# Weights of the last stage split sooner, one unit's weight sums on VectorE, and tokens loaded ahead of weights

## The chip, the cores and the metric

The kernel runs on one core of a Trainium2 chip. The metric is device time in microseconds, the median of several executions of the whole program; lower is better. Times inside the program come from one profiled execution, counted in us from the start of its span.

## What is computed

```python
scores = q @ k.T / sqrt(64) - log(448)         # 8 x 12 heads, 448 x 64 each, fp32
x = sigmoid(scores) @ v                        # tokens: 8*448 = 3584, features: 12*64 = 768
h = maximum(maximum(x @ w1, x @ w2), x @ w3)   # each w is 768 x 768
out = h @ w_out                                # 768 x 768
```

Everything is fp32. The weights arrive as 64-bit patterns (`w123`, `wout`), which the kernel decodes itself.

## The kernel before

First comes the attention (up to about 260 us), then the four products with weights. The change touches only the second part, at the step to its last stage.

The second part is a list of 16 **visits** (`visits`): four **stages** (three for column blocks of w1, w2 and w3, with the maximum taken among the three; the fourth, `LAST`, is w_out) times four **pairs** of batches. A visit has three **units** (q = 0, 1, 2), each a product of a 768 x 256 piece of weights with 768 x 896 tokens, done in Strassen's manner (Winograd's form): seven block **products** (k = 0 to 6, `PRODUCTS`) on 2 x 2 blocks. I write (n, q, k) for visit, unit, product, as the code does. Visit 12 is the first of the last stage.

A product (`product`, line 439 before) is nine matmuls 128 x 128 by 448. fp32 accuracy comes from splitting each operand in a rounded part and a remainder: three blocks of the contraction times `whi*xhi`, `whi*xlo` and `wlo*xhi`. So every operand needs a cast on ScalarE (`whi`, `xhi`) and a subtraction on VectorE (`wlo`, `xlo`, lines 154 and 264). The operands of the seven products are partly sums: of weights, `s1` to `s4` (`W_SUMS`, `w_combine`), and of tokens, `t1` to `t4` (`x_combine`, line 229, three 448-wide steps each). Both kinds of sum run on GpSimd. `s3` and `t3` overwrite the blocks a21 and b12.

Every engine's order is that of the program text (`pin`). What is done after which product stands in small tables with keys (n, q, k):

- `ws` says after which product a weight operand is split (`w_split`: cast, then remainder). Its list `when` has a row for each unit.
- `w_loads` says when the four weight blocks of a unit are loaded (`w_load`): unit 1 of the next stage where the last split of unit 0 stands, unit 2 where the last split of unit 1 stands. The loads go on SP's one queue, in the order a21, a22, a11, a12, and the four sums follow at the same place on GpSimd.
- `his` and `los` say when tokens are cast and when their remainder is taken; those of the next visit stand after the products of unit 2, and the last three after products of the next visit's unit 0.
- the tokens of the next visit are loaded by `x_load`: four loads on SP and then twelve steps on GpSimd. In the last stage this stands after (n, 0, 4), but in visit 12 after (12, 0, 6), behind the weight loads.

All staging tiles (`ws_*`, `xs_*`) and split tiles (`whi_*`, `wlo_*`, `xhi_*`, `xlo_*`) have one buffer each, so a load waits for the last reader of what it overwrites. The products accumulate in PSUM banks; bank 2 takes product 3 and again product 6 of a unit, and its results `m22` and `m12` are read by VectorE in between (`put`, line 511), before the bank is written again.

The line that sets the splits of unit 0, and the place of the token load:

```python
when = [[(n - 1, 1, 4 + k // 3) for k in range(7)],        # unit 0
        [(n, 0, 1)] * 2 + [(n, 0, 4)] * 2 + [(n, 0, 5)] * 2 + [(n, 0, 6)],   # unit 1
        [(n, 1, 4 + k // 3) for k in range(7)]]            # unit 2
...
if here == (n, 0, 6 if (n, 0, 6) in w_loads else 4) and nst in (0, LAST):
    xs = x_load(x_dram if nst == 0 else h_dram, np_)
```

Of the kernel before, what the change touches and what calls it, by code (L numbers as in the profile page):

```python
# [39 lines left out]
def attention_then_maxout(  # L40
# [31 lines left out]
    nc = tc.nc  # L72
# [8 lines left out]
    pin = tc.keep_in_program_order  # L81
# [52 lines left out]
        "s4": ("a12", "s2", ALU.subtract),  # L134
    }

    def w_combine(r, names):
        for name in names:
            r[name] = r["a21"] if name == "s3" else ws_p.tile([P, HP], F32, name=f"ws_{name}")
            in0, in1, op = W_SUMS[name]  # L140
            pin(nc.gpsimd.tensor_tensor(out=r[name], in0=r[in0], in1=r[in1], op=op))  # L141

    def w_load(st, q):
        r = w_stage()
        for name, sums in W_ORDER:
            pin(nc.sync.dma_start(out=r[name], in_=w_dram[st, q][:, BLOCKS.index(name)]))
        for name, sums in W_ORDER:
            w_combine(r, sums)
        return r

    def w_split(q, name, r, copy):
# [111 lines left out]
    def x_lo(name, x, hi, lo):  # L263
        pin(nc.vector.tensor_tensor(out=lo, in0=x, in1=hi.bitcast(F32), op=ALU.subtract))  # L264
        x_ops[name] = hi, lo
# [180 lines left out]
    pairs = list(range(B // 2))  # L446
# [7 lines left out]
    for n in range(1, done):  # L454
        (st0, p0), (st, p) = visits[n - 1], visits[n]
        if st != st0:
            if st < LAST:
                when = [[(n - 1, 1, k // 2) for k in range(7)],
                        [(n - 1, 2, 2 + k // 2) for k in range(7)],
                        [(n, 0, 3 + k // 2) for k in range(6)] + [(n, 1, 0)]]  # L460
            else:
                when = [[(n - 1, 1, 4 + k // 3) for k in range(7)],
                        [(n, 0, 1)] * 2 + [(n, 0, 4)] * 2 + [(n, 0, 5)] * 2 + [(n, 0, 6)],
                        [(n, 1, 4 + k // 3) for k in range(7)]]
            for q in range(3):
                for key, (name, _, _) in zip(when[q], PRODUCTS):
                    ws.setdefault(key, []).append((q, name))
            w_loads[n - 2, 0, 0] = st, 0
            w_loads[when[0][-1]] = st, 1
            w_loads[when[1][-1]] = st, 2  # L470
        if (st == LAST, p) != (st0 == LAST, p0):
            for k, (_, name, _) in enumerate(PRODUCTS):
                his[n - 1, 2, k] = name
            keys = [(n - 1, 2, k) for k in range(1, 5)] + [(n, 0, k) for k in (0, 2, 3)]
            for key, (_, name, _) in zip(keys, PRODUCTS):
                los[key] = name
    w_next, split = {}, {}
# [17 lines left out]
    for n, (st, p) in enumerate(visits):  # L495
        nst, np_ = visits[n + 1] if (n, 2, 0) in his else (None, None)
        if nst in (1, 2):
            xs = x_load_all(np_)
        m = {}
        for q in range(3):  # L500
            ps, p1, u2, u3 = {}, None, None, None

            def put(name, y, add):

                y = y[:, :S]
                if st == LAST or q == 0:
                    m[name] = m_p.tile([P, S], F32, name=f"m{name}")
                    if add is None:
                        pin(nc.scalar.copy(out=m[name], in_=y))  # L509
                    else:  # L510
                        pin(nc.vector.tensor_tensor(out=m[name], in0=y, in1=add, op=ALU.add))  # L511
                elif add is None:
                    pin(nc.vector.tensor_tensor(out=m[name], in0=y, in1=m[name], op=ALU.max))
                else:
                    c = c_p.tile([P, S], F32, name="c")
                    pin(nc.vector.tensor_tensor(out=c, in0=y, in1=add, op=ALU.add))
                    pin(nc.vector.tensor_tensor(out=m[name], in0=c, in1=m[name], op=ALU.max))  # L517
                if st == LAST or q == 2:
                    half, t = int(name[0]) - 1, (2 * p + int(name[1]) - 1) * S
                    if st == LAST:  # L520
                        row = (q + 3 * half) * P
                        dst = outT[row : row + P, t : t + S]
                    else:
                        dst = h_dram[half][:, st, t : t + S]
                    pin(nc.sync.dma_start(out=dst, in_=m[name]))

            for k, (wname, xname, bank) in enumerate(PRODUCTS):
                here = n, q, k
                first = k < 4 or bank == 1
                if first:  # L530
                    ps[bank] = ps_y.tile(
                        [P, 512], F32, name=f"ps_y{bank}", bufs=2 if bank < 2 else 1
                    )
                product(ps[bank], w_ops[q][wname], x_ops[xname], first)
                if k == 0:
                    p1 = c_p.tile([P, S], F32, name="p1", bufs=1)
                    pin(nc.scalar.copy(out=p1, in_=ps[0][:, :S]))  # L537
                elif k == 1:
                    u2 = c_p.tile([P, S], F32, name="u2", bufs=1)
                    pin(nc.vector.tensor_tensor(out=u2, in0=ps[1][:, :S], in1=p1, op=ALU.add))  # L540
                elif k == 2:
                    u3 = c_p.tile([P, S], F32, name="u3", bufs=1)
                    pin(nc.vector.tensor_tensor(out=u3, in0=ps[3][:, :S], in1=u2, op=ALU.add))
                elif k == 3:
                    put("22", ps[2], u3)
                elif k == 4:
                    put("11", ps[0], None)
                elif k == 5:
                    put("21", ps[1], u3)
                elif k == 6:  # L550
                    put("12", ps[2], u2)
                if here in his:
                    split[his[here]] = x_hi(his[here], x_first if n == q == 0 else xs)
                if here in los:
                    x_lo(*split.pop(los[here]))
                for uq, name in ws.get(here, ()):
                    w_split(uq, name, w_next[uq], nc.scalar.copy)
                if here in w_loads:
                    w_st, uq = w_loads[here]
                    w_next[uq] = w_load(w_st, uq)  # L560
                if here == (0, 0, 4):
                    finish(c_p, ("c", "c"))

                if here == (n, 0, 6 if (n, 0, 6) in w_loads else 4) and nst in (0, LAST):
                    xs = x_load(x_dram if nst == 0 else h_dram, np_)
                if here == (n, 2, 0) and nst == 0:
                    t_store(xs, np_)
                if here in decodes:
                    next(background)
# [41 lines left out]
```

## Time and profile before

| | us |
|---|---|
| median of 3 runs | 883.14 (882.99 to 884.2) |
| profiled execution, its own time | 882.73 |
| its span | 880.9 |
| TensorE busy | 870.7 |
| VectorE busy | 623.0 |
| ScalarE busy | 392.0 |
| GpSimd busy | 182.0 |

The span runs from the first to the last instruction of the profiled execution; its own time is a little longer. Busy time of matmuls includes their overlap with the next, so the spacing of matmul starts tells more than their duration. DVE is VectorE, ACT ScalarE, POOL GpSimd, PE TensorE, SP the engine that issues the DMAs.

### The profile page before, as it was taken

Reading aid. Unit: us, or ns where it says so; the run is one execution under the profiler, and the core shown is the slowest. Engines: PE = TensorE matmul, PEld = TensorE weight load, DVE = VectorE, ACT = ScalarE, POOL = GpSimd, SP = SyncE. Lnnn points to the kernel's source line nnn. Section 1 sums busy time; section 2 is a strip of 40 time slices with the busy share of each in tenths; the row PEclk is TensorE's granted clock in tenths of the full one; section 3 lists DMA queues with packets and bytes.
Section 4 is the critical chain, followed back from the end, with each engine's and each line's share of the span. In section 5 each row is a group of like instructions: output and inputs, shape, how many; then the busy total and the mean of one; then the engine's idle time right before and its main releaser. Section 6 shows DMA issues by size and latency. Waiting matters only on the chain. (4 is left out here: it accounts for less than half of the span.)

```text
span 880.9 us, 12944 instructions
## 1 busy us (share of the span) xinstructions
PE 870.7 (99%) x4842; PEld 693.3 (79%) x4842; DVE 623.0 (71%) x874; ACT 392.0 (45%) x499; POOL 182.0 (21%) x148
## 2 busy tenths in 40 slices
PE   8999999999999999999999999999999999999998
PEld 4444544444459999999999999999999998899997
DVE  4676668767866847678687788878778696836442
ACT  6777677766681413332353343235334252423320
POOL 0100022023003463502100010210001553760600
PEclk9999999999999999999999999999999999999999
DMA  6667666776747555314845642474472426162412
GB/s 244 214 230 231 228 242 208 245 274 224 232 162 259 184 202 193 147 51 152 296 161 192 242 147 81 153 283 179 173 270 100 157 74 219 72 210 93 170 72 84
DMA packets 74334, 161.87 MB, mean 184 GB/s; under 512 B 6944, under 2 KB 53792, under 8 KB 74272
## 3 DMA queue, kind: packets, MB, share of 16 engines
q1 hardware_dynamic: 74272, 161.05, 52.3%
q8 instruction: 38, 0.62, 0.3%
q14 instruction: 24, 0.20, 0.1%
HBM read 109.90 MB, written 51.12 MB: 183 GB/s over the span
## 5 line engine op out<-in xcount | busy, mean ns | idle before, releaser
L308 ACT ACTIVATE a<-ps_s,bias_s 128x896 f32<-128x896 f32 x168 | 156.1, 1007 | 77.9 <-PE ps_s L338 59.6
L439 PE MATMUL ps_y<-xhi_t,wlo_s 128*128 128x448 f32 x432 | 158.0, 366 | 0.1
L439 PE MATMUL ps_y<-xhi_t,whi_s 128*128 128x448 f32 x432 | 157.9, 366 | 0.0
L439 PE MATMUL ps_y<-xlo_t,whi_s 128*128 128x448 f32 x432 | 157.9, 366 | 0.0
L346 PE MATMUL ps_av<-a,v 128*64 128x448 f32 x576 | 118.6, 548 | 0.0
L439 PE MATMUL ps_y<-xhi_b,wlo_a 128*128 128x448 f32 x288 | 105.4, 366 | 0.0
L439 PE MATMUL ps_y<-xhi_b,whi_a 128*128 128x448 f32 x288 | 105.3, 366 | 0.0
L439 PE MATMUL ps_y<-xlo_b,whi_a 128*128 128x448 f32 x288 | 105.3, 366 | 0.0
L141 POOL TENSOR_TENSOR ws_s<-ws_a,ws_a 128x384 f32<-128x384 f32 x12 | 15.1, 1262 | 414.4 <-DMA ws_a<-w_dram 317.8
L537 ACT COPY p<-ps_y 128x448 f32<-128x448 f32 x48 | 25.5, 531 | 158.1 <-PE ps_y L439 158.1
L439 PEld LDWEIGHTS ps_y<-xhi_t,wlo_s 128*128 128x128 f32 x432 | 81.3, 188 | 6.7 <-ACT xhi_b L260 0.5
L439 PEld LDWEIGHTS ps_y<-xlo_t,whi_s 128*128 128x128 f32 x432 | 81.3, 188 | 6.3
L439 PEld LDWEIGHTS ps_y<-xhi_t,whi_s 128*128 128x128 f32 x432 | 81.2, 188 | 6.3
L346 PEld LDWEIGHTS ps_av<-a,v 128*64 128x64 f32 x576 | 37.2, 136 | 59.4 <-issue 58.2
L511 DVE TENSOR_TENSOR m<-ps_y,u 128x448 f32<-128x448 f32 x72 | 44.6, 620 | 54.7 <-PE ps_y L439 54.7
L229 POOL TENSOR_TENSOR xs_t<-xs_b,xs_t 128x448 f32<-128x448 f32 x48 | 64.5, 1369 | 35.3 <-DMA xs_b<-x_dram 34.2
L509 ACT COPY m<-ps_y 128x448 f32<-128x448 f32 x24 | 12.8, 533 | 126.3 <-PE ps_y L439 120.1
L264 DVE TENSOR_TENSOR xlo_t<-xs_t,xhi_t 128x1344 fp32r<-128x1344 f32 x42 | 67.7, 1612 | 1.9 <-ACT xhi_t L260 1.9
L540 DVE TENSOR_TENSOR u<-ps_y,p 128x448 f32<-128x448 f32 x48 | 29.9, 622 | 54.8 <-PE ps_y L439 53.6
L264 DVE TENSOR_TENSOR xlo_b<-xs_b,xhi_b 128x1344 fp32r<-128x1344 f32 x42 | 66.9, 1593 | 0.0
L260 ACT CAST xhi_t<-xs_t 128x1344 fp32r<-128x1344 f32 x42 | 55.5, 1322 | 16.3 <-PE ps_y L439 7.9
L175 ACT ACTIVATE c<-wraw 128x384 f32<-128x384 f32 x48 | 27.0, 562 | 76.9 <-DVE m L517 46.4
(65 smaller groups left out, 1629.0 us busy)
## 6 DMA issues: line engine op xcount, KB each, us to landing
qk<-qk SPq DMA_DIRECT2D x48, 448.0 KB, 5.2
xs_b<-x_dram SPq DMA_DIRECT2D x30, 672.0 KB, 6.8
wraw<-w SPq DMA_DIRECT2D x36, 384.0 KB, 4.9
xs_t<-t_dram SPq DMA_DIRECT2D x18, 672.0 KB, 8.0
v<-v SPq DMA_DIRECT2D x24, 448.0 KB, 3.8
h_dram<-m SPq DMA_DIRECT2D x48, 224.0 KB, 1.9
xs_b<-h_dram SPq DMA_DIRECT2D x16, 672.0 KB, 6.2
outT<-m SPq DMA_DIRECT2D x48, 224.0 KB, 1.9
```

Of the source, the lines that this page charges most:

```text
L141: pin(nc.gpsimd.tensor_tensor(out=r[name], in0=r[in0], in1=r[in1], op=op))
L175: pin(nc.scalar.activation(out=square, in_=high.bitcast(F32), func=AF.Square))
L229: pin(nc.gpsimd.tensor_tensor(out=r[name][:, k], in0=r[in0][:, k], in1=r[in1][:, k], op=ALU.subtract))
L260: pin(nc.scalar.copy(out=hi, in_=r[name]))
L264: pin(nc.vector.tensor_tensor(out=lo, in0=x, in1=hi.bitcast(F32), op=ALU.subtract))
L308: pin(nc.scalar.activation(out=a, in_=ps[:, :, :S], func=AF.Sigmoid, bias=bias_s, scale=scale))
L346: pin(nc.tensor.matmul(ps[e * D : (e + 1) * D, :S], vt[:, (g * C + c) * 2 + e], a[:, e], start=c == 0, stop=False,))
L439: pin(nc.tensor.matmul(ps[:, :S], wt[:, k * P : (k + 1) * P], xt[:, k], start=first and n == 0, stop=n == len(terms) - 1, skip_group_check ...
L509: pin(nc.scalar.copy(out=m[name], in_=y))
L511: pin(nc.vector.tensor_tensor(out=m[name], in0=y, in1=add, op=ALU.add))
L537: pin(nc.scalar.copy(out=p1, in_=ps[0][:, :S]))
L540: pin(nc.vector.tensor_tensor(out=u2, in0=ps[1][:, :S], in1=p1, op=ALU.add))
```

## The change

Four edits at the step to the last stage.

1. The splits of unit 0 of the last stage stand after (11, 1, 1) to (11, 1, 4) and not after (11, 1, 4) to (11, 1, 6). With them the weight load of unit 1, whose place is that of the last of these splits, goes from (11, 1, 6) to (11, 1, 4).
2. The weight load of unit 2 of the last stage comes without its sums (`combine=False`).
3. These four sums are VectorE's, after (12, 1, 3).
4. The tokens of visit 13 are loaded after (12, 0, 4), ahead of the weight load of unit 2 at (12, 0, 6).

```diff
-    def w_combine(r, names):
+    def w_combine(r, names, engine=None):
         for name in names:
             r[name] = r["a21"] if name == "s3" else ws_p.tile([P, HP], F32, name=f"ws_{name}")
             in0, in1, op = W_SUMS[name]
-            pin(nc.gpsimd.tensor_tensor(out=r[name], in0=r[in0], in1=r[in1], op=op))
-
-    def w_load(st, q):
+            engine = engine or nc.gpsimd
+            pin(engine.tensor_tensor(out=r[name], in0=r[in0], in1=r[in1], op=op))
+
+    def w_load(st, q, combine=True):
...
         for name, sums in W_ORDER:
-            w_combine(r, sums)
+            if combine:
+                w_combine(r, sums)
...
             else:
-                when = [[(n - 1, 1, 4 + k // 3) for k in range(7)],
+                when = [[(n - 1, 1, 1 + k // 2) for k in range(7)],
...
+                if here == (done - len(pairs), 1, 3):
+                    for name in W_SUMS:
+                        w_combine(w_next[2], (name,), nc.vector)
...
-                    w_next[uq] = w_load(w_st, uq)
+                    w_next[uq] = w_load(w_st, uq, (w_st, uq) != (LAST, 2))
...
-                if here == (n, 0, 6 if (n, 0, 6) in w_loads else 4) and nst in (0, LAST):
+                if here == (n, 0, 4) and nst in (0, LAST):
```

How this moves instructions stands in the two programs' orders. The names carry a running number at their end; `wlo_a11_0` is the remainder of block a11 for unit 0.

VectorE in unit 1 of visit 11, before:

```order
L540 TENSOR_TENSOR u2_6806<-ps_y1_6796,p1_6794 128x448
L543 TENSOR_TENSOR u3_6818<-ps_y3_6808,u2_6806 128x448
L516 TENSOR_TENSOR c_6830<-ps_y2_6820,u3_6818 128x448
L517 TENSOR_TENSOR m22_6724<-c_6830,m22_6724 128x448
L513 TENSOR_TENSOR m11_6736<-ps_y0_6784,m11_6736 128x448
L154 TENSOR_TENSOR wlo_a11_0_6844<-ws_a11_6361,whi_a11_0_6843 128x384
L154 TENSOR_TENSOR wlo_s2_0_6848<-ws_s2_6371,whi_s2_0_6847 128x384
L154 TENSOR_TENSOR wlo_s3_0_6852<-ws_a21_6363,whi_s3_0_6851 128x384
```

and now:

```order
L542 TENSOR_TENSOR u2_6806<-ps_y1_6796,p1_6794 128x448
L156 TENSOR_TENSOR wlo_a11_0_6809<-ws_a11_6361,whi_a11_0_6808 128x384
L156 TENSOR_TENSOR wlo_s2_0_6813<-ws_s2_6371,whi_s2_0_6812 128x384
L545 TENSOR_TENSOR u3_6826<-ps_y3_6816,u2_6806 128x448
L156 TENSOR_TENSOR wlo_s3_0_6829<-ws_a21_6363,whi_s3_0_6828 128x384
L156 TENSOR_TENSOR wlo_s1_0_6833<-ws_s1_6369,whi_s1_0_6832 128x384
L518 TENSOR_TENSOR c_6846<-ps_y2_6836,u3_6826 128x448
L519 TENSOR_TENSOR m22_6724<-c_6846,m22_6724 128x448
L156 TENSOR_TENSOR wlo_a12_0_6850<-ws_a12_6362,whi_a12_0_6849 128x384
L156 TENSOR_TENSOR wlo_a22_0_6854<-ws_a22_6364,whi_a22_0_6853 128x384
```

The remainders of unit 0 stand between the results of products 1 to 4 (`u2`, `u3`, `c`, `m22`), where they stood behind `m11` of product 4.

SP's queue from the first store of visit 12 on, before:

```order
L525 DMA outT<-m22_7080 128x448
L525 DMA outT<-m11_7093 128x448
L525 DMA outT<-m21_7114 128x448
L525 DMA outT<-m12_7134 128x448
L146 DMA ws_a21_7143<-w_dram32_98 128x384
L146 DMA ws_a22_7144<-w_dram32_98 128x384
L146 DMA ws_a11_7141<-w_dram32_98 128x384
L146 DMA ws_a12_7142<-w_dram32_98 128x384
L218 DMA xs_b11_7156<-h_dram0_66 128x3x448
L218 DMA xs_b12_7158<-h_dram0_66 128x3x448
L218 DMA xs_b22_7160<-h_dram1_67 128x3x448
L218 DMA xs_b21_7162<-h_dram1_67 128x3x448
```

and now:

```order
L527 DMA outT<-m22_7080 128x448
L527 DMA outT<-m11_7093 128x448
L220 DMA xs_b11_7104<-h_dram0_66 128x3x448
L220 DMA xs_b12_7106<-h_dram0_66 128x3x448
L220 DMA xs_b22_7108<-h_dram1_67 128x3x448
L220 DMA xs_b21_7110<-h_dram1_67 128x3x448
L527 DMA outT<-m21_7137 128x448
L527 DMA outT<-m12_7157 128x448
L147 DMA ws_a21_7166<-w_dram32_98 128x384
L147 DMA ws_a22_7167<-w_dram32_98 128x384
L147 DMA ws_a11_7164<-w_dram32_98 128x384
L147 DMA ws_a12_7165<-w_dram32_98 128x384
```

The four token loads have gone ahead of two stores and of the four weight loads.

VectorE from the end of product 3 of unit 1 in visit 12, before:

```order
L511 TENSOR_TENSOR m22_7225<-ps_y2_7215,u3_7213 128x448
L154 TENSOR_TENSOR wlo_a11_2_7241<-ws_a11_7141,whi_a11_2_7240 128x384
L154 TENSOR_TENSOR wlo_s2_2_7245<-ws_s2_7151,whi_s2_2_7244 128x384
L154 TENSOR_TENSOR wlo_s3_2_7249<-ws_a21_7143,whi_s3_2_7248 128x384
L511 TENSOR_TENSOR m21_7262<-ps_y1_7252,u3_7213 128x448
L154 TENSOR_TENSOR wlo_s1_2_7266<-ws_s1_7149,whi_s1_2_7265 128x384
```

and now:

```order
L513 TENSOR_TENSOR m22_7218<-ps_y2_7208,u3_7206 128x448
L142 TENSOR_TENSOR ws_s1_7221<-ws_a21_7166,ws_a22_7167 128x384
L142 TENSOR_TENSOR ws_s2_7223<-ws_s1_7221,ws_a11_7164 128x384
L142 TENSOR_TENSOR ws_a21_7166<-ws_a11_7164,ws_a21_7166 128x384
L142 TENSOR_TENSOR ws_s4_7226<-ws_a12_7165,ws_s2_7223 128x384
L156 TENSOR_TENSOR wlo_a11_2_7241<-ws_a11_7164,whi_a11_2_7240 128x384
L156 TENSOR_TENSOR wlo_s2_2_7245<-ws_s2_7223,whi_s2_2_7244 128x384
L156 TENSOR_TENSOR wlo_s3_2_7249<-ws_a21_7166,whi_s3_2_7248 128x384
L513 TENSOR_TENSOR m21_7262<-ps_y1_7252,u3_7206 128x448
```

The four sums stand ahead of the first remainder of unit 2's weights.

## Rows read from the trace of the kernel before

**Rows 1.** The head of the page: the span, and the busy time, share of the span and instructions of TensorE.

```profile
span 880.9 us, 12944 instructions
...
PE 870.7 (99%) x4842; PEld 693.3 (79%) x4842; DVE 623.0 (71%) x874; ACT 392.0 (45%) x499; POOL 182.0 (21%) x148
```

**Rows 2.** Who waited for whom, TensorE's matmuls alone, from 690 us to the end: us in total, times, longest us.

```profile
PE ps_y L439 <- DVE m L511: 1.4, 1, 1.4
PE ps_y L439 <- DVE xlo_t L264: 1.0, 1, 1.0
```

**Rows 3.** TensorE in order of time: start, duration, line, operation, operands; in brackets the idle time before and what ended it. The first matmul of visit 11, of visit 12, of unit 2 of visit 12, then the one with the longest wait, and the first of visits 13 and 14.

```profile
681.68 0.37 PE L439 MATMUL ps_y<-xhi_b,wlo_a 128*128 128x448 f32 x1
...
719.98 0.36 PE L439 MATMUL ps_y<-xhi_b,wlo_a 128*128 128x448 f32 x1
...
746.93 0.36 PE L439 MATMUL ps_y<-xhi_b,wlo_a 128*128 128x448 f32 x1
...
759.41 0.48 PE L439 MATMUL ps_y<-xhi_b,wlo_s 128*128 128x448 f32 x1 [1.38 <-DVE m L511]
...
761.36 0.36 PE L439 MATMUL ps_y<-xhi_b,wlo_a 128*128 128x448 f32 x1
...
800.48 0.36 PE L439 MATMUL ps_y<-xhi_b,wlo_a 128*128 128x448 f32 x1
```

**Rows 4.** VectorE in order of time, same columns: four remainders of visit 12's tokens (b11, t3, t1, t4).

```profile
713.26 1.55 DVE L264 TENSOR_TENSOR xlo_b<-xs_b,xhi_b 128x1344 fp32r<-128x1344 f32 x1
...
718.40 2.37 DVE L264 TENSOR_TENSOR xlo_t<-xs_b,xhi_t 128x1344 fp32r<-128x1344 f32 x1
...
721.23 1.83 DVE L264 TENSOR_TENSOR xlo_t<-xs_t,xhi_t 128x1344 fp32r<-128x1344 f32 x1
...
728.84 1.55 DVE L264 TENSOR_TENSOR xlo_t<-xs_t,xhi_t 128x1344 fp32r<-128x1344 f32 x1
```

**Rows 5.** SP in order of time, same columns, issues next to each other put together: visit 12's first four stores, unit 2's weight loads, the tokens of visit 13; then the tokens of visit 14.

```profile
730.94 4.74 SPq L525 DMA_DIRECT2D outT<-m  x4
...
735.77 1.83 SPq L146 DMA_DIRECT2D ws_a<-w_dram  x4
...
737.66 3.40 SPq L218 DMA_DIRECT2D xs_b<-h_dram  x4
...
772.63 2.73 SPq L218 DMA_DIRECT2D xs_b<-h_dram  x4
```

**Rows 6.** GpSimd in order of time, same columns: the first of unit 2's weight sums, the first and the last three token steps for visit 13, the first three for visit 14.

```profile
738.96 1.02 POOL L141 TENSOR_TENSOR ws_s<-ws_a,ws_a 128x384 f32<-128x384 f32 x1 [17.32 <-DMA ws_a<-w_dram]
...
745.89 4.01 POOL L229 TENSOR_TENSOR xs_t<-xs_b,xs_b 128x448 f32<-128x448 f32 x3 [2.40 <-DMA xs_b<-h_dram]
...
759.78 4.71 POOL L229 TENSOR_TENSOR xs_t<-xs_b,xs_t 128x448 f32<-128x448 f32 x3
...
779.32 3.36 POOL L229 TENSOR_TENSOR xs_t<-xs_b,xs_b 128x448 f32<-128x448 f32 x3 [14.83 <-DMA xs_b<-h_dram]
```

**Rows 7.** VectorE in order of time, same columns: remainders of unit 2's weights in visit 12 and the `m12` behind two of them.

```profile
744.50 0.56 DVE L154 TENSOR_TENSOR wlo_a<-ws_a,whi_a 128x384 fp32r<-128x384 f32 x1 [2.22 <-ACT whi_a L153]
...
747.38 2.93 DVE L154 TENSOR_TENSOR wlo_a<-ws_a,whi_a 128x384 fp32r<-128x384 f32 x2
...
750.24 0.61 DVE L511 TENSOR_TENSOR m<-ps_y,u 128x448 f32<-128x448 f32 x1
```

**Rows 8.** VectorE in order of time, same columns: results of products 2 and 3 of unit 1 of visit 11, the remainders of a12 and a22 of unit 0, and the result of product 1 of unit 2.

```profile
700.12 0.62 DVE L543 TENSOR_TENSOR u<-ps_y,u 128x448 f32<-128x448 f32 x1 [1.14 <-PE ps_y L439]
...
701.94 0.62 DVE L516 TENSOR_TENSOR c<-ps_y,u 128x448 f32<-128x448 f32 x1 [1.20 <-PE ps_y L439]
...
710.13 1.02 DVE L154 TENSOR_TENSOR wlo_a<-ws_a,whi_a 128x384 fp32r<-128x384 f32 x2
...
712.73 0.62 DVE L540 TENSOR_TENSOR u<-ps_y,p 128x448 f32<-128x448 f32 x1
```

**Rows 9.** GpSimd in order of time, same columns: the first and the last three token steps for visit 12, and the first weight sum of unit 1.

```profile
692.86 3.38 POOL L229 TENSOR_TENSOR xs_t<-xs_b,xs_b 128x448 f32<-128x448 f32 x3 [24.96 <-DMA xs_b<-h_dram]
...
703.70 4.44 POOL L229 TENSOR_TENSOR xs_t<-xs_b,xs_t 128x448 f32<-128x448 f32 x3
...
713.81 1.88 POOL L141 TENSOR_TENSOR ws_s<-ws_a,ws_a 128x384 f32<-128x384 f32 x1 [5.67 <-DMA ws_a<-w_dram]
```

**Rows 10.** ScalarE in order of time, same columns: the copy that gives m11 in unit 0 of visit 12.

```profile
729.30 0.53 ACT L509 COPY m<-ps_y 128x448 f32<-128x448 f32 x1 [5.94 <-PE ps_y L439]
```

**Rows 11.** DMA issues of a narrow stretch: destination and source, how many, KB each, median us from issue to landing. Issued at 772.63, 773.25 and 774.61 (tokens), at 775.76 and 776.21 (stores), from 653.82 to 655.42 (weights, behind token loads).

```profile
xs_b<-h_dram SPq DMA_DIRECT2D x1, 672.0 KB, 4.6
...
xs_b<-h_dram SPq DMA_DIRECT2D x1, 672.0 KB, 5.9
...
xs_b<-h_dram SPq DMA_DIRECT2D x1, 672.0 KB, 8.3
...
outT<-m SPq DMA_DIRECT2D x2, 224.0 KB, 7.8
...
ws_a<-w_dram SPq DMA_DIRECT2D x4, 192.0 KB, 8.9
```

**Rows 12.** Busy time by stretch: TensorE, its weight loads, VectorE, ScalarE and GpSimd, each with its instructions; then the granted TensorE clock, the share of the DMA engines, GB/s.

```profile
702.00:730.00 28.00, 27.46 (x136) 25.14 (x134) 27.79 (x33) 11.74 (x13) 13.89 (x9) 1.00 0.19 62
757.80:759.40 1.60, 0.24 (x2) 0.00 (x0) 1.56 (x2) 0.00 (x0) 1.60 (x1) 1.00 0.00 0
```

## The prediction

> **What bounds the kernel now.** I read the page first: TensorE is busy 870.7 of 880.9 us [rows 1], so a change to the order of side work can only give back, or take, time in which TensorE stands still. Next the waits of TensorE from 690 us on: only two of any size are left, one for VectorE's x remainders (`xlo`, 1.0) and one for a VectorE result `m` (1.4) [rows 2]. Then the start of each visit on TensorE [rows 3]. A visit is 3 x 7 x 9 = 189 matmuls. The visit at 681.68 lasts 38.30 (719.98 - 681.68); so a unit, a third of it, is 12.77 and a product, a seventh of that, 1.82. The visit at 719.98, the first of the last stage, lasts 41.38 and the next 39.12. All that can be won is 3.08 + 0.82 = 3.90 us. It splits in three: **A**, visit 12 before its unit 2: 746.93 - (719.98 + 25.54) = 1.41; **B**, inside unit 2: 761.36 - 746.93 - 12.77 = 1.66, nearly all of it the wait at 759.41; **C**, visit 13: 0.82.
>
> Why A: VectorE is late. The remainder of t4 starts at 728.84 and takes 1.55 [rows 4]; TensorE wanted it with the second matmul of product 5, at 719.98 + 9.12 + 0.20 = 729.30. Why B and C: GpSimd starts the token sums of visit 13 at 745.89 and ends them at 764.49, because the tokens' loads stand behind unit 2's weight loads and GpSimd first does that unit's four sums at 738.96 [rows 5, 6].
>
> **A contention that every term needs.** A VectorE subtraction of two SBUF tensors takes 0.55 when GpSimd rests, and two in a row 1.02, so 0.47 from one to the next; while GpSimd works, two take 2.93 and the instruction behind them begins 2.86 after the first, 1.43 each [rows 7, 8]. GpSimd's 448-wide step is 1.11 alone (3.36 for three at 779.32) and slower beside VectorE: 4.01 for the three at 745.89 [rows 6]. VectorE's operations with a PSUM input stay at 0.61 to 0.62 in the middle of this [rows 7, 8]. So the two engines take turns where both work on SBUF alone.
>
> **Edit 1, the seven splits of unit 0 three products sooner.** Nothing is added; seven VectorE remainders move, and ScalarE's order stays as it is. VectorE now idles 1.14 and 1.20 before its operations at 700.12 and 701.94; the moved remainders fill that, but GpSimd's twelve token steps run there (692.86 to 708.14), so they cost 1.43 and not 0.47 [rows 8, 9]. Of the 2.34 I therefore keep only some 0.7: VectorE reaches its operation of 712.73 at about 712. A second effect is larger. The remainder of a22 ends near 708 in place of 711.15, so the next weights' second load goes out 3 us sooner, and GpSimd's weight sums start near 710.6 in place of 713.81 [rows 9]. They are then over before the long remainders at 718.40 (2.37) and 721.23 (1.83), which fall to 1.55; the one at 713.26 gets slower by about 0.3 [rows 4]. Net 0.82 + 0.28 - 0.3 = 0.8. Together VectorE is 1.4 to 1.5 earlier at t4, which needs 1.1: **A goes, -1.41**. Bounds: 0 (all of the idle is eaten by contention) to -1.41, all there is.
>
> **Edit 2, tokens before weights.** Four loads go ahead of two stores and four weight loads on SP's queue. ScalarE's m11 is ready at 729.83 [rows 10]; with VectorE no longer late SP can issue its store at 729.9 and the first token load near 730.4 (today its four loads begin at 737.66 [rows 5]). Landings I take from the same four loads in visit 13, begun at 772.63: 4.6 after the first issue, 6.5 (issued at 773.25, 5.9), then about 8.4, and 10.3 (issued at 774.61, 8.3) [rows 5, 11]. That gives 735.0, 736.9, 738.8 and 740.7. GpSimd starts at 736.9 in place of 745.89 and no longer has the four sums. Twelve steps end by 752.4 even with contention (below), in place of 764.49: **B and C go, -2.48**. The two stores passed over land near 742, and the `m` tiles that they empty are written again only by unit 1, after 743.
>
> **What that does to the weights.** Loads land in the order of issue: two stores behind the tokens in visit 13 take 7.8 (the first lands at 783.5, 0.6 after the last token load), and four weight loads issued behind token loads in visit 10 take 8.9 [rows 11]. So unit 2's weights now come behind 740.7: two stores at 0.6 each, then four loads at 0.5 each (in visit 10 four were issued 0.5 apart and needed 8.9 in the median): a21 at 742.4, **a22 at 742.9**, a11 at 743.4, a12 at 743.9. Today the first sum begins at 738.96, so the pair was there by then.
>
> **Edit 3, the sums on VectorE.** GpSimd loses 4 x 1.02 [rows 6]; VectorE gains four operations, and behind them in its queue stand unit 2's seven remainders, the first of which TensorE needs at 719.98 + 25.54 = 745.52. The first sum can't start before 742.9. GpSimd is then in the middle of its twelve steps: 736.9 plus five at 1.11 is 742.5, and the other seven at 1.43 run to 752.4. So all five operations, four sums and the remainder of a11, go at 1.43: 742.9 + 5 x 1.43 = 750.1. **TensorE stands from 745.5 to 750.1: +4.6.** Bounds from both sides: five at 0.47 give 745.3, no wait; if the first sum gets its turn at once the chain is 0.96 shorter, 749.1; if VectorE is as late as today the loads start 1.4 later and the end is 751.5. I take 750.1, since the rows of 747.38 are the same form beside the same GpSimd steps.
>
> Behind that: the next remainders follow at 1.43 and TensorE asks for one each 1.82, so no new wait; m21 stands between, then at 0.47 each the rest. Unit 1's m12, which frees the PSUM bank that the fourth product of unit 2 overwrites, ends near 755.4; TensorE comes there at 750.1 + 5.47 = 755.6. That is a margin of 0.2.
>
> **Sum.** -1.41 - 1.66 - 0.82 + 4.6 = **+0.7**. The profiled execution took 882.73, so 883.4; the median of the runs, 883.14, lies 0.41 higher, so 883.8. With the bounds of the chain (749.1 to 751) it is 882.8 to 884.7. A change under 0.2% (1.77 us) can't be told from none here; the forecast is no change.
>
> **Rivals.**
> 1. *The sums don't meet GpSimd (faster).* If VectorE's five operations ran at 0.47, unit 2 would start on time and the whole 3.9 come back: 879.2. For it: a weight sum is 1.02 on GpSimd, and the same width 0.55 on VectorE [rows 6, 7]. Against it: GpSimd has twelve steps from 736.9 and can't be through before 736.9 + 13.3 = 750.2. The Trainium skill (GPSIMD Engine Reference, section 4.1) puts elementwise work on VectorE and calls GpSimd about half as fast for two inputs; the resting rows agree, 1.02 to 0.55. By that rule alone the sum would be this rival's. Chance 0.09.
> 2. *TensorE's clock falls in the wait (slower).* The longest wait today is 1.38, and the granted clock of the stretch around it is 1.00 [rows 3, 12]; a wait of 4.6 is more than three times that and has no counterpart in the trace after the start. If the first product or two after it ran at 1.2 in place of 2.4 GHz, 9 to 18 matmuls would each take 0.20 more (the pitch is 38.30 / 189 = 0.203): +1.8 to +3.7, that is 885.6 to 887.5. It decides once the wait is long enough, and no row says where that is. The Trainium skill (TensorE: Matmul & The Clock Gate, section "What's actually happening") states that an idle TensorE falls back to the lower clock and gets the higher one only after it has been busy again. No run here shows it yet. By that rule the sum would be this rival's, 885.6 at least. Chance 0.20.
> 3. *VectorE stays late (slower).* If edit 1 wins nothing against GpSimd, the token loads start 1.4 later, the weights too, and unit 2 begins at 751.5, not 746.93: 4.6 - 2.48 = +2.1, 885.2. For it: from 702 to 730 VectorE is busy for 27.79 of 28 us today [rows 12], and the moved work meets a busy GpSimd. Chance 0.12.
> 4. *The bank's margin of 0.2 is missed (slower).* One more contended turn (1.43) before m12 makes +1.2 of it: 885.0. Chance 0.07.
>
> **How the numbers follow.** Forecast 0.52; faster 0.09; slower 0.20 + 0.12 + 0.07 = 0.39. Time 883.8. The range goes from 882.2, a little under the chain's lower bound, to 887.0, which takes in rivals 3 and 4 and most of 2; it leaves out rival 1 and the dearest end of 2.
>
> **What would show it.** Unit 2 of visit 12 starts near 750 after an idle time of 4 to 5 us, ended by VectorE's remainder of a11; the five operations before it take 1.4 to 1.5 each; no wait at t4 in visit 12 and none in visit 13; GpSimd's token steps of visit 13 start near 737; weights land after the tokens. I am wrong if GpSimd rests when the sums run, if the weights land before 741, if the granted clock falls, or if a wait at unit 2's fourth product follows.

## The result and the profile after

The changed kernel takes 888.84 us in the median of 22 runs (885.61 to 892.78), the kernel before 883.92 in 22 runs on the same chips; the ratio is 1.0051 [1.0042, 1.006], without two runs of the kernel before that took 1073.9 and 1077.57. So it is slower by 0.5%, where no change was forecast, and outside the range (882.2 to 887.0). The profiled execution took 886.43, with a span of 884.4 (880.9 before [rows 1]).

The head of the page after:

```profile
span 884.4 us, 12945 instructions
...
PE 871.9 (99%) x4842; PEld 695.5 (79%) x4842; DVE 626.9 (71%) x878; ACT 392.8 (44%) x499; POOL 175.9 (20%) x144
```

Who waited for whom, TensorE's matmuls from 690 us to the end: us in total, times, longest us.

```profile
PE ps_y L441 <- DVE wlo_a L156: 4.2, 1, 4.2
```

Both waits of [rows 2] are gone, and one new one is there. TensorE in order of time, after (columns as in [rows 3]): the starts of visits 12, 13 and 14, and what lies around unit 2 of visit 12.

```profile
720.83 0.36 PE L441 MATMUL ps_y<-xhi_b,wlo_a 128*128 128x448 f32 x1
...
746.16 0.36 PE L441 MATMUL ps_y<-xhi_b,whi_s 128*128 128x448 f32 x1
750.73 0.74 PE L441 MATMUL ps_y<-xhi_b,wlo_a 128*128 128x448 f32 x1 [4.20 <-DVE wlo_a L156]
751.27 0.58 PE L441 MATMUL ps_y<-xlo_b,whi_a 128*128 128x448 f32 x1
...
755.00 0.51 PE L441 MATMUL ps_y<-xhi_t,whi_s 128*128 128x448 f32 x1
755.35 0.37 PE L441 MATMUL ps_y<-xhi_t,wlo_s 128*128 128x448 f32 x1
...
765.69 0.37 PE L441 MATMUL ps_y<-xhi_b,wlo_a 128*128 128x448 f32 x1
...
804.00 0.36 PE L441 MATMUL ps_y<-xhi_b,wlo_a 128*128 128x448 f32 x1
```

Visit 13 lasts 38.31 (39.12 before), visit 12 44.86 (41.38 before) [rows 3]. Unit 2 was due at 720.83 + 25.54 = 746.37 and starts at 750.73: 4.36 late. And the matmuls behind the wait are slow: the matmuls from 750.73 to 755.35 are 13, twelve spacings in 4.62 and not in 12 x 0.203 = 2.43, which is 2.19 more. The granted clock says why. Busy time by stretch, after (start, end and length; TensorE, its weight loads, VectorE, ScalarE, GpSimd, each with its instructions; the granted clock, DMA share, GB/s):

```profile
746.35:748.49 2.14, 0.18 (x1) 0.00 (x0) 2.14 (x3) 1.10 (x3) 2.14 (x2) 1.00 0.00 0
748.49:750.70 2.21, 0.00 (x0) 0.00 (x0) 2.21 (x3) 1.57 (x4) 2.21 (x3) 0.50 0.00 0
750.70:755.31 4.61, 4.58 (x12) 4.16 (x13) 4.61 (x6) 0.76 (x2) 2.39 (x2) 0.50 0.09 33
755.31:765.00 9.69, 9.69 (x49) 8.99 (x49) 9.22 (x11) 7.59 (x7) 0.00 (x0) 1.00 0.22 81
```

TensorE is idle from 746.5 on; at 748.49 the clock falls to 0.50 (1.2 GHz) and it is back at 1.00 (2.4 GHz) from 755.31.

What ended the wait, VectorE in order of time: t4's remainder, the four sums (L142), the remainder of a11, and m12.

```profile
728.25 1.55 DVE L266 TENSOR_TENSOR xlo_t<-xs_t,xhi_t 128x1344 fp32r<-128x1344 f32 x1
...
743.76 1.27 DVE L142 TENSOR_TENSOR ws_s<-ws_a,ws_a 128x384 f32<-128x384 f32 x1 [2.04 <-DMA ws_a<-w_dram]
745.06 1.40 DVE L142 TENSOR_TENSOR ws_s<-ws_s,ws_a 128x384 f32<-128x384 f32 x1
746.38 1.48 DVE L142 TENSOR_TENSOR ws_a<-ws_a,ws_a 128x384 f32<-128x384 f32 x1
747.79 1.48 DVE L142 TENSOR_TENSOR ws_s<-ws_a,ws_s 128x384 f32<-128x384 f32 x1
749.20 1.48 DVE L156 TENSOR_TENSOR wlo_a<-ws_a,whi_a 128x384 fp32r<-128x384 f32 x1
...
755.37 0.61 DVE L513 TENSOR_TENSOR m<-ps_y,u 128x448 f32<-128x448 f32 x1
```

GpSimd's twelve token steps for visit 13 run through all of it, after:

```profile
737.91 3.37 POOL L231 TENSOR_TENSOR xs_t<-xs_b,xs_b 128x448 f32<-128x448 f32 x3 [19.39 <-DMA xs_b<-h_dram]
741.23 3.38 POOL L231 TENSOR_TENSOR xs_t<-xs_b,xs_t 128x448 f32<-128x448 f32 x3
744.57 4.29 POOL L231 TENSOR_TENSOR xs_b<-xs_b,xs_b 128x448 f32<-128x448 f32 x3
748.82 4.26 POOL L231 TENSOR_TENSOR xs_t<-xs_b,xs_t 128x448 f32<-128x448 f32 x3
```

Three steps take 3.37 while VectorE has no sums and 4.29 beside them; [rows 6] had 3.36 and 4.01 for the two cases. They end at 753.08, where those of before ended at 764.49. SP's queue, after: tokens, two stores, weights.

```profile
731.26 2.81 SPq L220 DMA_DIRECT2D xs_b<-h_dram  x4
734.17 1.21 SPq L527 DMA_DIRECT2D outT<-m  x2
735.48 2.66 SPq L147 DMA_DIRECT2D ws_a<-w_dram  x4
```

**The account of the two profiled executions.** The span grew by 3.5: 0.28 because the weight products begin later (260.50 for 260.22), 0.58 in visit 6 (38.88 for 38.30, behind a wait of 0.3 for VectorE), 4.36 for the wait, 2.19 for the clock, less the 3.08 + 0.82 of before: 0.28 + 0.58 + 4.36 + 2.19 - 3.90 = 3.51. The median is 2.4 above this execution; that is for the experiments.

### The profile page after: what moved, and what is told of

Read it like the earlier page. It is cut to its first block, busy times and chain, and to the rows that moved or that the text cites. A ratio compares the mean times of both kernels' runs of the same rounds, so it can differ in the third digit from the quotient of the medians.

```text
span 884.4 us, 12945 instructions
## 1 busy us (share of the span) xinstructions
PE 871.9 (99%) x4842; PEld 695.5 (79%) x4842; DVE 626.9 (71%) x878; ACT 392.8 (44%) x499; POOL 175.9 (20%) x144
## 4 chain that ended last, share of the span: by engine, by line
PE 92%; DMA 3%; DVE 2%; issue 1%; SPq 0%; ACT 0%; DVEq 0%
PE ps_y L441 63%; PE ps_av L348 13%; PE ps_s L328 11%; PE ps_av L357 2%; PE ps_s L340 2%; DMA xs_b<-x_dram 1%; DMA ws_a<-w_dram 1%; DMA w_dram<-wb 1%; DMA qk<-qk 0%; DVE c L518 0%; SPq L252 0%; DVE m L519 0%; DVE ws_s L142 0%; DVE wb L183 0%; DVE xlo_t L266 0%
## 5 line engine op out<-in xcount | busy, mean ns | idle before, releaser
L142 POOL TENSOR_TENSOR ws_s<-ws_a,ws_a 128x384 f32<-128x384 f32 x11 | 13.3, 1211 | 390.3 <-DMA ws_a<-w_dram 294.6
L266 DVE TENSOR_TENSOR xlo_t<-xs_t,xhi_t 128x1344 fp32r<-128x1344 f32 x42 | 65.7, 1565 | 0.0
L231 POOL TENSOR_TENSOR xs_t<-xs_b,xs_b 128x448 f32<-128x448 f32 x24 | 27.4, 1165 | 179.8 <-DMA xs_b<-h_dram 98.7
L441 PEld LDWEIGHTS ps_y<-xhi_b,wlo_a 128*128 128x128 f32 x288 | 54.6, 189 | 9.5 <-DVE wlo_a L156 4.6
```

The costliest lines, as they stand in the source:

```text
L142: pin(engine.tensor_tensor(out=r[name], in0=r[in0], in1=r[in1], op=op))
L231: pin(nc.gpsimd.tensor_tensor(out=r[name][:, k], in0=r[in0][:, k], in1=r[in1][:, k], op=ALU.subtract))
L441: pin(nc.tensor.matmul(ps[:, :S], wt[:, k * P : (k + 1) * P], xt[:, k], start=first and n == 0, stop=n == len(terms) - 1, skip_group_check ...
```

## The experiments

Theory: the walk through the queues was right (+0.5), and the rest is what the long wait does to TensorE afterwards. Rivals: the weights land late, whoever else works; the other edits cost something of their own. The line numbers differ by a few between the kernels.

**What the wait costs beyond its length.** *e4_busy* and *e4_again* (the same kernel) fill the wait with useless work; *e5_some* and *e5_again* fill less of it:

```diff
+                if here == (done - len(pairs), 1, 6):
+                    idle = ps_av.tile([P, 512], F32, name="ps_av0")
+                    for n_idle in range(20):        # 8 in e5
+                        pin(nc.tensor.matmul(idle[:, :S], w_ops[1]["s4"][1][:, :P],
+                                             x_ops["b22"][1][:, 0], start=True, stop=True))
```

> The changed kernel with 20 extra matmuls (their result is never read) between unit 1 and unit 2 of visit 12, where TensorE otherwise stands still; 20 x 0.203 = 4.1 us of extra work. Theory (the wait, then the clock): VectorE's remainder of a11 is as late as before, so unit 2 still starts about 4.4 us late, but TensorE is not idle, the granted clock stays 1.00 and the time is about 0.5 to 1 us over the kernel before, some 4 us under the changed kernel. Rival (the loss is spread over waits that the edits cause on VectorE, GpSimd and the DMA queue, the clock is a by-product): the extra work costs 0 to 4 us, so at least as slow as the changed kernel, 4.5 us or more over the kernel before.

Measured: 885.78 (12 runs), ratio to before 1.0013 [0.9995, 1.003], below the interval of the change (1.0042 to 1.006); by the medians it is 1.8 over before, where 0.5 to 1 was expected. Unit 2 starts at 750.85, 4.64 after its due time and so as late as in the change, and no stretch of matmuls is at half the clock. The wait, now filled, and what follows it (columns as above):

```profile
746.50:750.85 4.35, 4.34 (x22) 3.69 (x21) 4.35 (x5) 2.68 (x6) 4.35 (x4) 1.00 0.00 0
750.85:756.00 5.15, 5.15 (x25) 4.70 (x26) 5.15 (x7) 2.83 (x3) 2.39 (x2) 1.00 0.13 45
```

So 4 us of extra matmuls make the kernel faster by some 3 us: that part of the loss is TensorE's idleness, not the late weights. It does not rest on the profiled executions alone, since every run lists its mean granted clock: 0.999 or 1.000 in the 12 runs here, 0.995 to 0.998 in all 22 of the change (0.996 in the profiled execution), and 0.998 or less in 6 of the 71 runs of the kernel before that were made beside the experiments.

But visits 13 to 15, with no wait in them, took 39.06 each in this execution and not 38.30. Hence a second execution:

> The changed kernel with 20 unused matmuls in the wait, once more. Theory (the matmuls hold the clock, the pitch after the restart is chosen anew in each execution): granted clock 1.00 throughout, visit 12 of 43.3; visits 13 to 15 either 38.30 each, time about 883.5 to 884.5, or 39.06 each, about 886 to 887. Rival (the unused matmuls themselves make the slow pitch): 39.06 again.

Measured: 884.84 (0.3 above the band), clock 1.00, visit 12 of 43.38, visits 13 to 15 of 38.30. The rival (the unused matmuls make the slow pitch) is out: here they stand before visits of 38.30, and *a1* below has the slow ones without them.

> The changed kernel with 8 extra matmuls in the wait before unit 2 of visit 12 (20 in the run before), so that about 2.7 us of idle time are left of 4.4. Theory: 2.7 us is still near what the kernel before had without a fall (1.4); clock 1.00 and the same time as with 20 extra matmuls, 1 to 2 us over the kernel before. Rival (any idle time of more than 2 us lets the clock fall): low-clock matmuls at 0.374 after the wait and the changed kernel's time, 4.5 us over the kernel before.

Measured: 886.79 (12 runs, 883.62 to 892.35), ratio 1.0034 [1.0015, 1.0052], 2.4 over before by the medians and so between the two forecasts (1 to 2, and 4.5). The profiled execution (884.9) is one without a fall of the clock. Its TensorE wait from 690 us on, and two stretches of it (columns as above):

```profile
PE ps_y L441 <- DVE wlo_a L156: 3.1, 1, 3.1
```

```profile
746.50:751.40 4.90, 1.85 (x11) 1.37 (x9) 4.90 (x5) 2.67 (x6) 4.90 (x5) 1.00 0.00 0
751.40:756.00 4.60, 4.60 (x23) 4.28 (x24) 4.60 (x6) 2.36 (x3) 2.37 (x2) 1.00 0.09 34
```

A wait of 3.1, and the clock stays at 1.00.

> The changed kernel with 8 unused matmuls in the wait, once more. Theory (8 matmuls hold the clock in some executions only): either the clock stays 1.00 and visit 12 lasts 43.3, or it falls to 0.50 for 3 to 7 us and visit 12 lasts 44.5 to 45.6; visits 13 to 15 at 38.30 or 39.06. Time 884 to 889 by these.

Measured: 883.88, a wait of 2.7, clock 1.00 again, visit 12 of 42.96, visits 13 to 15 of 38.30. Both profiled executions are without a fall, but six of the twelve runs of *e5_some* list a mean clock of 0.997 or 0.998, the other six 0.999 or 1.000: by this, 8 matmuls hold the clock in some executions only. Runs of 888 and more are in both halves; none of them was profiled.

*a1* is the changed kernel once more.

> The changed kernel once more, one execution with its profile. Theory: the wait before unit 2 of visit 12 is 4.2 to 4.6 us again and a stretch at clock 0.5 follows; what differs between executions (885.6 to 892.8) is how long that stretch lasts and the pitch at which TensorE goes on behind it (visits of 38.30 or of 39.06). Rival: the wait itself differs from execution to execution by some us.

Measured: 889.32. The wait is the same (4.58 from start to start, 4.57 in the other), the clock is 0.50 from 749.5 to 756.3, and visits 13 to 15 take 39.06 each. Its span is 887.4, 3.0 more than that of the execution of the result: 3 x 0.76 = 2.28 in visits 13 to 15, 0.74 in visit 12 (45.60), and +0.36 and -0.38 ahead of them. The low stretch of *a1*:

```profile
749.50:756.30 6.80, 5.48 (x15) 4.87 (x16) 6.80 (x9) 2.31 (x4) 3.68 (x3) 0.50 0.09 34
```

The same 40 us of undisturbed visits in the execution of the result, then in *a1*:

```profile
806.00:846.00 40.00, 40.00 (x199) 37.11 (x199) 19.80 (x23) 12.78 (x14) 13.38 (x12) 1.00 0.40 141
```

```profile
806.00:846.00 40.00, 40.00 (x196) 36.32 (x195) 20.77 (x24) 13.19 (x14) 13.38 (x12) 1.00 0.40 140
```

The clock is 1.00 in both, and three matmuls fewer fit.

**The edits apart.** *e1_splits* has edit 1 alone, *e13* edits 1 and 3 with the tokens behind the weights as before, *e23* all but edit 1. The numbers are the prediction's: its edit 2 (tokens before weights) is number 4 in the list of the change, its edit 3 (the sums) is numbers 2 and 3 there.

```diff
# e1_splits, against before
-                when = [[(n - 1, 1, 4 + k // 3) for k in range(7)],
+                when = [[(n - 1, 1, 1 + k // 2) for k in range(7)],
# e13, against the change
-                if here == (n, 0, 4) and nst in (0, LAST):
+                if here == (n, 0, 6 if (n, 0, 6) in w_loads else 4) and nst in (0, LAST):
# e23, against the change
-                when = [[(n - 1, 1, 1 + k // 2) for k in range(7)],
+                when = [[(n - 1, 1, 4 + k // 3) for k in range(7)],
```

> Edit 1 alone: unit 0's splits after (11,1,1) to (11,1,4). Theory: the wait A in visit 12 (1.4 us at t4) goes, B and C stay, no wait of 4 us, clock 1.00: 1.4 us under the kernel before (0.16%). Rival (the moved remainders meet GpSimd's token steps and win nothing): within 0.3 us of the kernel before, with the wait at t4 still in the trace.

Measured: 883.52, ratio 0.999 [0.9969, 1.0011], no difference that can be told. The wait at t4 shrinks (0.56 from start to start, 1.34 before) but does not go, as it was expected to; the one at (12,2,6) is 2.01 (1.74 before). Edit 1 alone gives part of A.

> Edits 1 and 3, not the tokens: unit 2's weights are loaded ahead of the tokens as in the kernel before, and their four sums are VectorE's. Theory: the weights land near 739 as before, GpSimd rests then, the sums take 0.55 each, unit 2 starts on time; 1.4 us under the kernel before, as with edit 1 alone, B and C still there. Rival (sums on VectorE are the trouble wherever the tokens stand): a wait of 2 us or more before unit 2, over the kernel before.

Measured: 883.04, ratio 0.9983 [0.9965, 1.0001], 0.9 under before by the medians where 1.4 was expected. The sums on VectorE cost nothing here, because GpSimd rests until 745.59. VectorE in *e13*:

```profile
742.37 0.55 DVE L142 TENSOR_TENSOR ws_s<-ws_a,ws_a 128x384 f32<-128x384 f32 x1
742.95 0.56 DVE L142 TENSOR_TENSOR ws_s<-ws_s,ws_a 128x384 f32<-128x384 f32 x1
743.43 0.55 DVE L142 TENSOR_TENSOR ws_a<-ws_a,ws_a 128x384 f32<-128x384 f32 x1
743.90 0.55 DVE L142 TENSOR_TENSOR ws_s<-ws_a,ws_s 128x384 f32<-128x384 f32 x1
```

No matmul waits at the start of unit 2. But GpSimd's token steps start at 745.59 in place of 745.89 [rows 6]: without edit 2 the loads set their start, not the sums, and B (1.74) and C (0.51) stay. Edit 3 is neither loss nor gain until edit 2 puts the token steps beside it.

> Edits 2 and 3 without edit 1: the splits of unit 0 stand where they stood. Theory: the wait at t4 (1.2 to 1.4 us) is back and everything behind it, token loads, weights and sums, is later by that; unit 2 of visit 12 starts 1.2 us later than in the changed kernel, the wait of over 4 us before it and the fall of the clock are there: 1 to 1.5 us over the changed kernel. Rival (edit 1 causes the wait by crowding VectorE): no wait of over 2 us before unit 2, under the changed kernel.

Measured: 888.13, ratio 1.0047 [1.0022, 1.0071], as slow as the whole change: wait 4.61 from start to start, clock 0.50 from 761.0 to 764.4. The 1 to 1.5 over the change that were expected are not there: the profiled execution has no wait at t4, and unit 2 starts 4.63 after its due time (4.36 in the change). Its visits 0 to 11 took 39.06 each, hence its span of 893.6; the pitch changed at 741.8, ahead of the wait, and visits 13 to 15 took 38.30.

**The turns taken elsewhere.** *g1* keeps the tokens first and puts the four sums back on GpSimd, ahead of the token steps. *m4_apart* lets VectorE do s1, s2 and the first two remainders before GpSimd may start:

```diff
# g1, order on GpSimd
+ (12,0,6): sums s1, s2, s3, s4, then t1, t2, t3, t4      # weights' sums ahead of the tokens'
# m4_apart
+ (12,1,3): VectorE s1, s2; GpSimd s4, then t1, t2, t3, t4
+ (12,1,4): VectorE remainders of a11 and s2, then sum s3; the other remainders one product later
```

> The changed kernel's queue order (tokens loaded ahead of unit 2's weights, edit 1 kept), but unit 2's four sums on GpSimd, ahead of the token steps. The sums then meet no token steps and unit 2 starts on time; the token steps come later than in the changed kernel, so waits return inside unit 2 (about 2 us at its fourth and 3 us at its last product) and in visit 13 (under 1): by the walk some 5 to 6 us of standing still in all, against 4.6 in the changed kernel, but in pieces. Theory (one long wait lets the clock fall, and that is the greater part of the loss): clock 1.00, 1.5 to 2.5 us over the kernel before, 2 to 3 us under the changed kernel. Rival (the time goes with the sum of the waits, whatever their length): 1 us or more over the changed kernel.

Measured: 887.87 (6 runs), ratio 1.0048 [1.0029, 1.0067], 3.4 over before by the medians where 1.5 to 2.5 was expected. The waits are in pieces, 2.43 at (12,2,3), 1.50 at (12,2,6) and 0.50 at (13,0,3) from start to start; that the clock would hold with shorter waits was wrong, and all six runs list a mean clock of 0.997 or 0.998. *g1* in four stretches, the wait in the second:

```profile
748.00:751.60 3.60, 3.60 (x19) 3.29 (x18) 3.48 (x4) 3.38 (x7) 3.60 (x3) 1.00 0.17 64
751.60:754.10 2.50, 0.44 (x3) 0.05 (x1) 2.50 (x4) 0.00 (x0) 2.50 (x3) 1.00 0.00 0
754.10:754.80 0.70, 0.70 (x3) 0.67 (x4) 0.70 (x1) 0.00 (x0) 0.70 (x2) 1.00 0.00 0
754.80:758.20 3.40, 3.40 (x11) 3.00 (x11) 3.08 (x4) 0.00 (x0) 3.40 (x2) 0.50 0.21 72
```

Here the clock falls after the wait, when TensorE has been at work again for 0.7.

> The changed kernel with the five operations kept apart from GpSimd: VectorE does the sums s1 and s2 after (12,1,3) and then at once the remainders of a11 and s2; the sum s3 follows behind them after (12,1,4); the sum s4 stands on GpSimd, ahead of the twelve token steps, so that these can't start before VectorE's s2 is there. Loads as in the change. Theory (the wait of 4.6 is five turns against GpSimd's token steps): the first sum still starts near 743 to 744, s1, s2 and the remainder of a11 take 0.5 to 0.6 each, unit 2 of visit 12 starts within 0.3 of its due time. The token steps then run from 744 to 762 and the turns are paid there: waits of about 1 at (12,2,3) and 2 to 2.3 at (12,2,6), in all some 3.5 to 4.5, as much as the one wait of the change. With the clock at 1.00 that is 882.5 to 885, at a restart at the slow pitch 2.5 more. Rival (the sums are late because the weights land late, whoever else works): unit 2 starts near 750 as in the change.

Measured: 885.41 (884.42 to 891.78, 10 runs), ratio 1.0015 [0.9985, 1.0044]; 0.4 above the forecast band. VectorE and GpSimd in *m4_apart*, then TensorE's two waits:

```profile
744.25 0.56 DVE L141 TENSOR_TENSOR ws_s<-ws_a,ws_a 128x384 f32<-128x384 f32 x1 [2.09 <-DMA ws_a<-w_dram]
744.85 0.56 DVE L141 TENSOR_TENSOR ws_s<-ws_s,ws_a 128x384 f32<-128x384 f32 x1
745.32 0.55 DVE L154 TENSOR_TENSOR wlo_a<-ws_a,whi_a 128x384 fp32r<-128x384 f32 x1
```

```profile
745.53 1.21 POOL L141 TENSOR_TENSOR ws_s<-ws_a,ws_s 128x384 f32<-128x384 f32 x1 [26.72 <-DVE ws_s L141]
```

```profile
753.48 0.47 PE L439 MATMUL ps_y<-xhi_t,wlo_s 128*128 128x448 f32 x1 [0.82 <-DVE m L513]
...
761.18 0.47 PE L439 MATMUL ps_y<-xhi_b,wlo_s 128*128 128x448 f32 x1 [1.86 <-DVE m L513]
```

The weights land as late as in the change (744.25), and yet the remainder of a11 is through at 745.87 and unit 2 starts without a wait (at 746.92, 0.56 after its due time, half of that by small waits at t4, half by the slow pitch told of below). Two operations fewer stand ahead of this remainder than in the change; two more at 0.47 would, by estimate, have ended at 746.81, still before unit 2 began. So the 4.36 belong to the turns against GpSimd, and the rival (weights landing late) is out. The turns are then paid at products 3 and 6 of unit 2, 1.19 and 2.23 from start to start, and visit 13 takes 39.11: over 38.30 visits 12 and 13 lose 4.84 in pieces, the slow pitch included, where the change had 4.36 in one. The clock stays 1.00 in the profiled execution, but five of the ten runs list a mean clock of 0.997 or 0.998.

**Another timetable.** *best1* spreads the loads and the sums:

```diff
+ unit 0's splits from (11,0,6) on, unit 1's from (12,0,0), unit 2's from (12,1,4) to (12,2,0)
+ loads: tokens b11, b12 after (12,0,1); a21 after (12,0,3); a22, a11 after (12,0,5);
+        b22, a12 after (12,0,6); b21 after (12,2,1)
+ GpSimd: s1, t1 after (12,0,6); s4 after (12,1,0); t3, t2, t4 after (12,1,1), (12,1,6), (12,2,3)
+ VectorE: s2 after (12,0,6), s3 after (12,1,1)
```

> Edit 1's idea with another timetable for the step to the last stage: the tokens b11 and b12 of visit 13 are loaded after (12,0,1), unit 2's weights between (12,0,3) and (12,0,6), each as soon as its staging tile is free, b22 behind them and b21 after (12,2,1); two of the four weight sums on GpSimd (s1, s4) and two on VectorE (s2, s3), ahead of most token steps; the splits of units 0 and 1 spread one per product where VectorE has room. Theory (all that the kernel before loses here are late operands at TensorE): no wait left in visits 12 and 13, clock 1.00, 3.9 us under the kernel before (0.44%). Rival (the moved work only moves the waits, as in the changed kernel): 1.4 us under at best, with waits of over 1 us left.

Measured: 879.72 (878.71 to 887.56, 12 runs) beside 884.42 of before, ratio 0.9962 [0.9942, 0.9982]; it beats both kernels. TensorE's waits in it from 700 us on:

```profile
PE ps_y L439 <- DVE m L513: 0.7, 1, 0.7
```

Visit 12 takes 39.25 and visit 13 38.30; that is 2.13 + 0.82 = 2.95 of the 3.90 won; a wait of 0.7 is left where none was forecast. Its token loads start earlier in part, and two sums are on VectorE in place of four, over at 739.93 and not at 749.27; which of its moves wins how much was not taken apart.

**The kernel before once more.**

> The kernel before once more. If the two pitches of TensorE belong to every kernel, this execution shows either 38.30 in every undisturbed visit (time about 882.5 to 883.5) or 39.06 from some restart on (0.76 more for each such visit); the waits in visits 12 and 13 stay as they were (1.3, 1.7, 0.5 start to start) and the granted clock 1.00. A visit of another length than 38.30 or 39.06 without a wait in it would be against it.

Measured: 882.95, all undisturbed visits 38.30, clock 1.00, waits of 1.76 and 0.49 as before and 0.87 at t4 (1.34 in the first execution). No series at the slow pitch was seen in either profiled execution of this kernel.

## Why the prediction was wrong

**What was right.** A, B and C are gone: t4's remainder ends 8.97 after the start of visit 12 (10.41 before; 1.44 earlier, and 1.4 to 1.5 was forecast), visit 13 is free of waits, and GpSimd begins at 737.91. Counted from the start of visit 12, the first token step was forecast at 16.9 and came at 17.1, the first sum at 22.9 and 22.9, the end of a11's remainder at 30.1 and 29.85. Five turns at 1.43 were 7.15; they took 6.92. The wait came to 4.36 for 4.6. m12 ended at 755.98, ahead of product 3, so rival 4 did not come; nor did rival 3. The walk alone gives 4.36 - 3.90 = +0.46 where +0.7 stood. One reserve: A is gone in both executions of the change, but *e1_splits*, *e13* and *e4_again* still show 0.56 to 0.57 there (spacing of matmul starts), *e4_busy* and *g1* 0.34 and 0.35. So edit 1's gain has no margin, and that A goes whole in the profiled execution is in part luck. One slip in the sum: the chain's upper bound is worked out as 751.5 and then used as 751, so 884.7 should read 885.2; nothing hangs on it.

**The step that failed** is the sum: it let the long wait cost its length and no more, and left the clock to a rival with a chance of 0.20. The wait is more than three times the longest of before, which the text said itself; the clock fell in both profiled executions of the change and in the one of *e23*, and by the mean clocks in all 22 runs of the change. There 12, 15 and 9 matmuls ran at half the clock, and the price was 2.19 in the execution of the result, 2.63 in *a1* and 1.66 in *e23*, where the rival had 1.8 to 3.7. The Trainium skill (TensorE: Matmul & The Clock Gate, section "What's actually happening") has this fall of an idle TensorE; the trace agrees here, with 0.50 from 748.49 on. The length of a wait alone does not decide it: *e5_some* and *e5_again* had 3.1 and 2.7 of idle time in the profiled executions and kept the clock at 1.00, *g1* had 2.07 and lost it.

**The term that was missing** is the pitch after a restart. The low clock explains the profiled 886.43, not the median of 888.84. In *a1* the visits behind the wait are 0.76 longer each, 2.28 in all. The runs of the change fall apart accordingly: 8 of 22 between 885.6 and 887.2, the other 14 between 888.39 and 892.78. The clock does not part the two groups, since both have runs of 0.996. That most of the 14 have the slow pitch to the end is argued, not shown run by run: of seven profiled executions with the wait before unit 2, two (*a1* and *e4_busy*) went on at the slow pitch. With rival 2's price and this one the sum is 883.8 + 2.2 + 2.3 = 888.3; the range ended at 887.0 because it held the first of them only. The measured terms, 0.46 + 2.19 + 2.28 = 4.93, come to what lies between the medians (4.92); that they fit so closely is luck, since the third is one execution's.

What stays open: what picks the pitch, why a wait of 2.07 (*g1*) was followed by a fall of the clock and one of 3.1 (*e5_some*) was not, and why filling the wait won some 3 by the medians, more than the 1.66 to 2.63 that the low clock cost in the profiled executions.

## What to carry to other kernels

Price a wait of TensorE at its length and at what follows. Where a long one can't be avoided, useless matmuls in it can pay. Cutting it in pieces is no sure way out: *m4_apart* came to 885.41, but *g1*, in pieces too, to 887.87, beside 888.84 for the change. Before moving work from a slow engine to a fast one, look at what else the slow one will do at that time: two engines that take turns give the moved work the slow one's pace, and the turns come back at another place when only their order is changed.

## What the runs showed of the hardware

**TensorE has two pitches at the same granted clock of 1.00**: 0.2027 (visits of 38.30) and 0.2066 to 0.2067 (visits of 39.06). It changed mostly where a matmul had waited, but not only there: in *e13* at 706.2 and in *g1* at 748.6 no spacing near the change is over 0.209, and in *e23* at 741.8 it is 0.214. Worked out from the starts: start of a series at one pitch, matmuls in it, mean spacing.

```
m4_apart   261.4 x2314 0.2027   732.5 x97 0.2066   761.5 x35 0.2065   775.3 x511 0.2027
e13        261.2 x2196 0.2027   706.2 x63 0.2066   732.9 x124 0.2026   767.6 x18 0.2066   773.7 x511 0.2027
a1         732.3 x70   0.2027   756.5 x615 0.2067
e23        261.7 x2322 0.2067   742.0 x69 0.2027   764.5 x618 0.2027
g1         718.5 x54   0.2066   732.1 x81 0.2027   748.6 x16 0.2067   776.7 x511 0.2027
e4_busy    732.4 x70   0.2027   751.2 x629 0.2067
e4_again   732.8 x70   0.2027   751.6 x629 0.2027
```

After a wait, short ones too, it can be the other one, and the last change before a long undisturbed series counts most. This is also the likeliest cause of the spread of runs of one kernel (882.1 to 891.9 for the kernel before beside the experiments), which no profile of it shows: the three slowest of these 71 runs (890.67, 891.84, 891.92) list a mean clock of 1.000, so it is not the clock.

**The clock can fall after a wait as well as in it**: in the change at 748.49, with 2.2 of the wait still to come, in *g1* 0.7 and in *e23* 0.5 after it had ended. The low stretch lasted 6.8 in both executions of the change, 3.4 in *g1* and *e23*.

**It falls in some runs of a kernel and not in others, by and large more often behind longer waits.** The profiled executions with a fall list a mean clock of 0.995 to 0.998, those without one 1.000. Runs with a mean clock of 0.998 or less, and the longest idle time of TensorE from 690 us on in the kernel's profiled execution:

| | runs | idle us |
|---|---|---|
| e4_busy | 0 of 12 | filled |
| best1 | 0 of 12 | 0.7 |
| before | 6 of 71 | 1.4 |
| e13 | 3 of 12 | 1.4 |
| e1_splits | 3 of 12 | 1.6 |
| m4_apart | 5 of 10 | 1.9 |
| g1 | 6 of 6 | 2.1 |
| e5_some | 6 of 12 | 3.1 |
| e23 | 11 of 12 | 4.2 |
| the change | 22 of 22 | 4.2 |

The mean does not say where in a run the clock fell.
